# Moving one of two weighted-value sums to an earlier step, splitting a placement, and reordering the sums by bank, in a fused thresholded-attention and squared-ReLU kernel

## The chip, the core and the metric

The kernel runs on one core of one Trainium2 chip. The metric is device time in microseconds (us), the median of repeated runs; lower is better. The core has a matrix engine (PE), a vector engine (DVE), a scalar engine (ACT), a general-purpose engine (POOL), a queue that only issues transfers (SP), and 16 DMA engines. Each engine works through its own instructions in the order of the program, and waits on semaphores for the others.

## What is computed

```python
scores = 0.125 * q @ k^T                       # 8 batches x 8 heads, 576 x 576, head_dim 64
scores = where(scores >= rowmax(scores) - tau, scores, -1e9)
attn   = exp(scores - rowmax) / sum            # softmax over what is kept
x      = (attn @ v), heads side by side        # 4608 x 512
out    = relu(x @ w_in)**2 @ w_out             # 512 -> 2048 -> 512
```

All data are float32.

## The kernel before

**Visits and steps.** The two heads of a pair share one *visit*; there are 32 pairs (8 batches of 4), and so 36 visits, as the first four pairs are visited twice. From visit 12 on, visits go two by two: an even visit n and the odd visit n+1 belong together, and make a *period* of nine *steps*. A step handles 128 query rows of both heads. Step s of a period holds the 64 leftover rows of both visits, steps s+1 to s+4 the blocks 0 to 3 of visit n, and steps s+5 to s+8 the blocks 0 to 3 of visit n+1. There are twelve such periods, run by `late_step`. The score matmuls of two blocks are done at once (L282), at s, s+1, s+3, s+5 and s+7.

**What a step does.** Scores into PSUM banks 0 to 4 (PE, L282); the row maximum (DVE, L303); the exponential (ACT, L318); threshold and sum (DVE, L330); division (POOL, L340). One step later, `turn_blocks` transposes the block in squares of 32 x 32 on DVE into one of two halves of the tile `turned` (L420). Then `place_blocks` has SP issue 16 transfers of 72 KB or 36 KB each that copy these squares to their places in `wT`, the transposed weights (L432 for the block pairs 0 and 1, L437 for the leftover rows). A placement is written (visit, 0), (visit, 1), or (n, 2) for the leftover rows. A period thus has five placements, 80 transfers, all on SP in program order.

**The value sums.** `mix` multiplies `wT` with the values `vs` (PE, L482): 20 matmuls that gather 320 columns in bank 0 (*one*) and 256 columns in bank 4 (*two*). *One* reads the columns ONE of `wT` (block pair 0) and a leftover strip next to them, LEFT for even visits and ODD for odd ones; *two* reads the columns TWO (block pair 1). `put` then copies the sums to `xT` on ACT (L469, L465). `wT` exists once: a placement into ONE has to wait until the last `mix` that reads ONE is done.

**The order around the change.** The step at which a `mix` runs is in `mixes`; the one at which a placement is issued is in `place_at`. In before, `mix` of visit n runs at the beginning of step s+8, and `mix` of n+1 at the beginning of s+11, which is s+2 of the next period. Placements: (n,2) at s+2, (n,0) at s+3, (n,1) at s+5, (n+1,0) at s+8, (n+1,1) at s+9.

**Filling.** All other time of PE goes to *pieces* of the second half of the computation, the two large products with `w_in` and `w_out` (L638, L744), each 1.76 us by the planner's constant `PIECE_US`. `rate` works out how many a step should take, and `fill` issues a quarter of them at a time. A step with a `mix` gets fewer pieces, by `VALUES_US`. An even step puts its scores first, then the turning, the maxima and pieces; an odd step its maxima, then a `mix` if there is one, the turning and pieces. The ring `xT` holds 1280 tokens, and `put` must not overwrite tokens that are still to be read (`read_to`).

Of the kernel before, what the change touches and what calls it, by code (L numbers as in the profile page):

```python
# [19 lines left out]
def kernel(  # L20
# [11 lines left out]
    B, H, S, D = q.shape  # L32
# [3 lines left out]
    HP = H // 2  # L36
    NPAIR = B * HP
    NBLK = S // P
# [51 lines left out]
    RING = 5 * TCH  # L90
# [105 lines left out]
    def some_loads():  # L196
        for _ in range(min(1 + (len(loads) > 8), len(loads))):
            to, src = loads.popleft()
            (nc.gpsimd if state["step"] > first_dma + 2 else nc.sync).dma_start(out=to, in_=src)

    def arrived(t):
        assert all(x[0].tensor.name != t.tensor.name for x in loads)
# [144 lines left out]
    def take(what, among):  # L347
        used[what] += 1
        return bank[among[used[what] % len(among)]]
# [98 lines left out]
    read_to = {"x": 0}  # L448
# [30 lines left out]
    def mix(n, cols):  # L479

        def term(ps, u, c, at, rows=slice(0, P), first=False, last=False):
            nc.tensor.matmul(ps[u * D:(u + 1) * D, :], vs[n % 2][rows, u * (NBLK + 1) + c, :],  # L482
                             wT[rows, NBLK if c == NBLK else u * (NBLK + 1) + c, at:at + ps.shape[1]],
                             start=first, stop=last)

        above, below = slice(0, D), slice(D, P)
        arrived(vs[n % 2])
        if not by_dma(n):
            ps = take("tx", (4, 5))[:, 0:cols.stop - cols.start]
            for c in range(NBLK):  # L490
                for u in range(2):
                    term(ps, u, c, cols.start, first=(c == 0))
            for u, rows in enumerate((above, below)):
                term(ps, u, NBLK, cols.start, rows, last=True)
            put(n, cols.start, ps, False)
            return
        n1, n2 = 2 * P + REST, 2 * P
        at = ODD if paired(n) and n % 2 else ONE
        one, two = bank[0], bank[4]
        groups = (one[:, 0:n1], at, (above, below)), (two[:, 0:n2], TWO, (below, above))  # L500
        for c in range(NBLK):
            for ps, x, _ in groups:
                for u in range(2):
                    term(ps, u, c, x, first=(c == 0))

        for ps, x, places in groups:
            for u, rows in enumerate(places):
                term(ps, u, NBLK, x, rows, last=True)
        put(n, 0, one[:, ONE - at:ONE - at + 2 * P], True)
        left = ODD if at == ODD else LEFT - at  # L510
        put(n, NBLK * P, one[:, left:left + REST], False)
        put(n, 2 * P, two[:, 0:n2], True)
# [85 lines left out]
    def some_later(engine):  # L598
        if later[engine]:
            make(*later[engine].popleft())  # L600
# [191 lines left out]
    visits = [(g_, list(range(FIRST))) for g_ in range(HP)] + [(g_, list(range(FIRST, NBLK + 1))) for g_ in range(HP)]  # L792
    visits += [(g_, list(range(NBLK + 1))) for g_ in range(HP, NPAIR)]

    def paired(n):

        return n >= 3 * HP
# [7 lines left out]
    def by_dma(n):  # L805

        return n >= 3 * HP - 1
# [5 lines left out]
    mixes = {}  # L813
    complete = {}
    for s, (n, i) in enumerate(steps):

        if by_dma(n):
            mixed = {visits[n][1][-1]: (0, 3 if n % 2 else 4)}
        else:
            mixed = {x: (x, 3) for x in range(NBLK + 1)}  # L820
        if i in mixed:
            first, lag = mixed[i]
            cols = slice(first * P, S if by_dma(n) else min((i + 1) * P, S))
            mixes[s + lag] = (n, cols)
            g_ = visits[n][0]
            if g_ % HP == HP - 1:
                complete[s + lag] = g_ // HP * S + cols.stop
    END = max(mixes)

    chunk_at, j = {}, 0  # L830
# [29 lines left out]
    def add_chunk(j):  # L860
        waiting.extend(pieces_of(j))
        whole.add(j)
# [25 lines left out]
    def after():  # L888
        now = state["last"]
        state["last"] = []  # L890
        for fn in state["then"]:
            state["last"] += fn() or []
        state["then"] = []
        for fn in now:
            fn()

    def piece():
        _, fn, *what = waiting.popleft()
        state["left"] -= PIECE_US
        if fn is mlp_out or what[0] <= PLAIN and what[1] == 0:  # L900
            after()
        then = fn(*what)
        after()
        state["then"] = then
        if state["step"] >= NST:
            some_later("vector")
            some_later("gpsimd")

    def fill(us):
        state["left"] += us  # L910
        while waiting and state["left"] >= PIECE_US / 2 and waiting[0][0] <= state["usable"]:
            piece()
        state["left"] = min(state["left"], PIECE_US)

    pieces, left = [], n_pieces
    for s, (n, i) in enumerate(steps):
        if s < HP * FIRST:
            x = int(n > 0 and i == 0)
        else:
            x = 2 if (n, i) in ((2 * HP - 2, FIRST + 1), (2 * HP - 1, FIRST + 1), (2 * HP, FIRST)) else 1  # L920
# [13 lines left out]
    place_at, load_at, prep_at = ({s: [] for s in range(END + 10)} for x in range(3))  # L934
    for s, (n, i) in enumerate(steps):
        if not by_dma(n) or i != visits[n][1][0] or paired(n) and n % 2:
            continue
        nxt = n + (2 if paired(n) else 1)
        more = nxt < len(visits)
        if paired(n):  # L940

            place_at[s + 2].append((n, 2))
            place_at[s + 3].append((n, 0))
            place_at[s + 5].append((n, 1))
            place_at[s + 8].append((n + 1, 0))
            place_at[s + 9].append((n + 1, 1))
            prep_at[s].append(lambda n=n: prep_part(q, n))
            load_at[s].append(lambda n=n: load_part(q, n + 1))
            load_at[s + 2].append(lambda n=n: load_v(n))
            prep_at[s + 4].append(lambda n=n: prep_part(q, n + 1))  # L950
            load_at[s + 4].append(lambda n=n: load_v(n + 1))
        else:
            place_at[s + 3].append((n, 0))
            place_at[s + 4].append((n, 1))
            place_at[s + 5].append((n, 2))
        if more:
            a, b, c, d = (s + 1, s + 5, s + 7, s + 8) if paired(n) else (s + 1, s + 2, s + 4, s + 4)
            load_at[a].append(lambda n=nxt: load_part(k, n))
            if paired(n):
                load_at[a].append(lambda n=nxt: load_left(n))  # L960
            prep_at[b].append(lambda n=nxt: prep_part(k, n))
            load_at[b].append(lambda n=nxt: load_part(k, n + 1))
            if not paired(n):
                load_at[s - 8].append(lambda n=nxt: load_left(n))
            load_at[b].append(lambda n=nxt: load_part(q, n))
            prep_at[c].append(prep_left)
            prep_at[d].append(lambda n=nxt: prep_part(k, n + 1))
# [16 lines left out]
    def turn_last(s):  # L984
        if s <= NST:
            turn_blocks(*steps[s - 1])
        for what in place_at[s]:
            place_blocks(*what)

    def late_step(s):  # L990

        on = s < NST
        odd = on and steps[s][1] % 2 == 1
        if on:
            n, i = steps[s]
            if not odd:
                scores_of_two(s)
                turn_last(s)
            maxima(s, [area(u, odd) for u in range(2)])
            after()  # L1000
            some_later("gpsimd")
            exponents(n, i)
        if s in mixes:
            mix(*mixes[s])
            for j in chunk_at.get(s, ()):
                add_chunk(j)
        if odd or not on:
            turn_last(s)
        quarter = rate(s) / 4 if s < END else 1e9
        fill(quarter)  # L1010
        some_later("vector")
        some_later("gpsimd")
        smooth = s not in mixes
        if smooth:
            after()
        if on:
            threshold(n, i)
            for fn in prep_at[s] + load_at[s]:
                fn()
            divide(n, i)  # L1020
        if smooth:
            fill(quarter)
            after()
            some_later("gpsimd")
        some_loads()
        some_later("vector")
        if not smooth:
            some_later("gpsimd")
            fill(quarter)
        some_loads()  # L1030
        fill(quarter)
        some_loads()
        fill(quarter)
        some_loads()

    for s in range(END + 1):
# [9 lines left out]
        if on:  # L1046
            n, i = steps[s]
# [49 lines left out]
        smooth = s > first_dma + 2 and s not in mixes  # L1097
# [23 lines left out]
        if 0 < s <= NST and by_dma(steps[s - 1][0]):  # L1121
            m, x = steps[s - 1]
# [57 lines left out]
```

## Time and profile before

The time is 1424.66 us, the median of 3 runs (1424.31 to 1427.45). The profiled execution spans 1423.4 us. Its stages on PE:

| stretch | length | PE busy | mean granted clock | what runs |
|---|---|---|---|---|
| 0 to 290 us | 290 us | 257.7 us | mixed | first visits, rounding of weights |
| 290 to 1273 us | 983 us | 920.2 us | 0.98 | the twelve periods, with pieces |
| 1273 to 1423 us | 150 us | 146.8 us | 1.00 | pieces alone |

The other engines in the middle stretch: DVE busy for 703.1 us, POOL for 718.9, ACT for 374.8. PE is the engine with the least idle time, and so the table is read from its side: in the middle stretch it stands for 62.8 us in which it does nothing, and the granted clock, a share of its full speed, shows whether it was slowed besides.

### The profile page before, as it was taken

The page shows a single profiled execution, that of the slowest core. Times are in us where ns is not written, and L with a number is a line of the kernel's source. Part 1 is how long each engine was busy: PE and PEld are TensorE (multiplying, and loading weights), DVE is VectorE, ACT ScalarE, POOL GpSimd, SP SyncE. Part 2 cuts the span into 40 slices and gives each one's busy share as a digit, 9 for nine tenths or more (in the row PEclk, how much of TensorE's full clock was granted, in tenths as well). Part 3 has the DMA queues.
Part 4 walks back from the last instruction along what each step waited for, and adds up shares of the span by engine and source line. Part 5 has one row for each costly group of instructions (what it writes and reads, how often), then busy time and mean ns, then how long its engine had stood idle before and what let it go on. Part 6 is the DMA issues. An engine that isn't in the chain of part 4 may idle for free.

```text
span 1423.4 us, 25861 instructions
## 1 busy us (share of the span) xinstructions
PE 1324.7 (93%) x9112; PEld 1092.6 (77%) x9112; DVE 949.0 (67%) x2026; ACT 582.5 (41%) x1357; POOL 976.4 (69%) x1229
## 2 busy tenths in 40 slices
PE   7899999799898989989998999989989998999998
PEld 5676567577686868778787878877777876889998
DVE  6877776667685877757886777858677767722232
ACT  4777673225252524325342444333425252513322
POOL 3688874696776859595978686868685766652451
PEclk8999999999999999999999999999999999999999
DMA  7754431444646555544646555454645436240000
GB/s 151 162 157 138 118 73 36 80 91 85 108 85 98 115 93 112 87 94 82 115 81 116 99 108 102 87 88 87 107 97 89 91 74 105 59 82 1 16 16 16
DMA packets 406354, 128.15 MB, mean 90 GB/s; under 512 B 390064, under 2 KB 394448, under 8 KB 406224
## 3 DMA queue, kind: packets, MB, share of 16 engines
q1 hardware_dynamic: 385632, 95.10, 37.3%
q0 software_dynamic: 18288, 31.11, 8.3%
q8 instruction: 72, 1.18, 0.4%
q10 hardware_dynamic: 2304, 0.29, 0.2%
q14 instruction: 58, 0.48, 0.1%
HBM read 50.59 MB, written 9.44 MB: 42 GB/s over the span
## 4 chain that ended last, share of the span: by engine, by line
PE 61%; SPq 13%; POOL 10%; DVE 5%; issue 4%; ACT 4%; DMA 3%; ACTq 0%; DVEq 0%; POOLq 0%
PE big L744 18%; PE big L638 18%; SPq L432 11%; PE big L482 10%; PE big L282 5%; PE big L530 3%; PE big L266 3%; DMA wT<-turned 3%; POOL w L340 2%; POOL g L569 2%; PE big L709 2%; PE big L380 2%; DVE w L330 1%; DVE st L303 1%; DVE turned L420 1%
## 5 line engine op out<-in xcount | busy, mean ns | idle before, releaser
L303 DVE TENSOR_REDUCE st<-big 128x1 f32<-128x576 f32 x288 | 203.5, 745 | 92.4 <-PE big L282 58.3
L420 DVE STREAM_TRANSPOSE turned<-w 128x512 f32<-128x512 f32 (+2 forms) x388 | 174.8, 499 | 122.1 <-POOL w L340 64.4
L340 POOL TENSOR_SCALAR w<-w,st 128x576 f32<-128x576 f32 x269 | 233.8, 878 | 24.0 <-DVE st L333 17.3
L330 DVE SCALAR_TENSOR_TENSOR w<-big,st,w 128x576 f32<-128x576 f32 x269 | 208.2, 810 | 56.8 <-ACT w L318 56.5
L744 PE MATMUL big<-wo,gsum 128*128 128x256 f32 x1088 | 244.5, 382 | 0.0
L482 PE MATMUL big<-wT,vs 128*64 128x128 f32 (+7 forms) x1700 | 189.1, 381 | 56.9 <-issue 28.2
L744 PEld LDWEIGHTS big<-wo,gsum 128*128 128x128 f32 x1088 | 204.5, 190 | 36.7 <-issue 9.5
L482 PEld LDWEIGHTS big<-wT,vs 128*64 128x64 f32 (+1 forms) x1700 | 107.6, 145 | 134.2 <-issue 77.6
L638 PE MATMUL big<-xT,w_in_sb 128*128 128x128 f32 x1536 | 187.7, 277 | 8.0 <-DVE g L650 6.4
L338 POOL TENSOR_SCALAR st<-st 128x2 f32<-128x2 f32 (+1 forms) x148 | 33.8, 229 | 234.3 <-DVE w L330 227.3
L638 PEld LDWEIGHTS big<-xT,w_in_sb 128*128 128x128 f32 x1536 | 179.1, 192 | 16.1 <-DVE g L650 7.7
L744 PE MATMUL big<-wo,g 128*128 128x256 f32 x816 | 186.2, 382 | 0.5 <-ACT g L646 0.5
L318 ACT ACTIVATE w<-big,st 128x576 f32<-128x576 f32 x269 | 183.6, 733 | 0.2 <-ACT st L316 0.2
L744 PEld LDWEIGHTS big<-wo,g 128*128 128x128 f32 x816 | 151.4, 190 | 27.3 <-issue 7.9
L315 ACT ACTIVATE st<-st 128x2 f32<-128x2 f32 (+1 forms) x148 | 30.2, 204 | 268.6 <-DVE st L303 267.5
L650 DVE TENSOR_TENSOR g<-big,g 128x512 f32<-128x512 f32 x96 | 64.7, 677 | 76.5 <-PE big L638 71.5
L282 PE MATMUL big<-kT,qT 64*128 64x256 f32 (+3 forms) x768 | 107.5, 416 | 0.7 <-DVE qT L240 0.6
L282 PEld LDWEIGHTS big<-kT,qT 64*128 64x128 f32 x768 | 84.7, 187 | 15.5 <-issue 7.5
L646 ACT ACTIVATE g<-g 128x512 f32<-128x512 f32 x96 | 60.5, 630 | 77.2 <-DVE g L650 77.1
L520 POOL TENSOR_TENSOR gsum<-g 128x512 f32<-128x512 f32 x34 | 44.2, 1301 | 61.0 <-ACT g L647 60.7
L647 ACT ACTIVATE g<-g 128x512 f32<-128x512 f32 x128 | 80.7, 630 | 4.1
L638 PE MATMUL big<-xT,gsum 128*128 128x128 f32 x512 | 65.1, 281 | 4.2 <-POOL gsum L569 3.8
(114 smaller groups left out, 2136.8 us busy)
## 6 DMA issues: line engine op xcount, KB each, us to landing
wT<-turned SPq DMA_DIRECT2D x800, 72.0 KB, 2.2
wo<-in_moe_w_in_dram SPq DMA_DIRECT2D x16, 512.0 KB, 4.5
wo<-in_moe_w_out_dram SPq DMA_DIRECT2D x16, 512.0 KB, 3.6
out_dram<-osb POOLq DMA_DIRECT2D x32, 256.0 KB, 2.5
ql<-in_q_dram POOLq DMA_DIRECT2D x96, 72.0 KB, 2.9
wT<-turned SPq DMA_DIRECT2D x192, 36.0 KB, 2.0
kl<-in_k_dram POOLq DMA_DIRECT2D x88, 72.0 KB, 3.0
vs<-in_v_dram POOLq DMA_DIRECT2D x48, 128.0 KB, 3.2
```

What stands on the lines that cost most here:

```text
L282: nc.tensor.matmul(big[to, at + x0:at + x1], lhsT, keys[u * D:(u + 1) * D, x0:x1], start=True, stop=True)
L303: nc.vector.tensor_reduce(out=mx[:, u:u + 1], in_=sc[u], axis=AX.XY, op=ALU.max)
L318: nc.scalar.activation(out=w[:, u, :].rearrange("p (h k) -> p h k", h=2), in_=sc[u], func=AF.Exp, bias=bias[:, u:u + 1], scale=SCALE)
L330: nc.vector.scalar_tensor_tensor(out=wu, in0=sc[u], scalar=thr[:, u:u + 1], in1=wu, op0=ALU.is_ge, op1=ALU.mult, accum_out=sm[:, u:u + 1])
L340: nc.gpsimd.tensor_scalar(out=w[:, u, :], in0=w[:, u, :], scalar1=z[:, u:u + 1], scalar2=rcp[:, u:u + 1], op0=ALU.add, op1=ALU.mult)
L420: nc.vector.transpose(wb[:, at:at + k1 - k0, i % 2, :], w[:, u, k0 * 32:k1 * 32].rearrange("p (k q) -> p k q", q=32))
L432: nc.sync.dma_start(out=to[:, :, at:at + 64], in_=wb[rows, j::4, :, :].rearrange("p c u q -> p c (u q)"))
L482: nc.tensor.matmul(ps[u * D:(u + 1) * D, :], vs[n % 2][rows, u * (NBLK + 1) + c, :], wT[rows, NBLK if c == NBLK else u * (NBLK + 1) + c, a ...
L638: nc.tensor.matmul(to[:, f, :], factor(j, p, q, c)[:, f * P:(f + 1) * P], part[:, c, :], start=(p in "125" and f == 0 and c == 0), stop=(p ...
L647: nc.scalar.activation(out=to, in_=to, func=AF.Square)
L650: nc.vector.tensor_tensor(out=x, in0=to, in1=x, op=ALU.add)
L744: nc.tensor.matmul(to, left[:, f, :], wo[:, slot, f, :], start=(f == 0), stop=(f == HF - 1))
```

## The change

Four edits. (1) `mix` of an even visit moves from the beginning of step s+8 to the end of step s+6, ahead of the last quarter of the pieces; the same place in its step is taken by `mix` of visit 11, the unpaired visit ahead of the periods. A loop ahead of it runs pieces until the ring `xT` has room. (2) Placement (n+1,0) moves from s+8 to s+7, right after the turning of its second block. (3) Placement (n,2) is split: the half that goes to LEFT is issued at s+1, the half that goes to ODD at s+2 (both at s+3 in the first period). (4) Within `mix`, all of *one*'s matmuls over the four whole key blocks are done ahead of *two*'s, in place of taking turns. The aim is that a transfer is issued as soon as its squares are turned.

```diff
-        for c in range(NBLK):
-            for ps, x, _ in groups:
+        for ps, x, _ in groups:
+            for c in range(NBLK):
                 for u in range(2):
                     term(ps, u, c, x, first=(c == 0))
...
-            mixed = {visits[n][1][-1]: (0, 3 if n % 2 else 4)}
+            mixed = {visits[n][1][-1]: (0, 3 if n % 2 else 2)}
...
-            place_at[s + 2].append((n, 2))
+            a, b = (1, 2) if paired(n - 1) else (3, 3)
+            place_at[s + a].append((n, 2, (0, 1)))
+            place_at[s + b].append((n, 2, (2, 3)))
...
-            place_at[s + 8].append((n + 1, 0))
+            place_at[s + 7].append((n + 1, 0))
...
-        if s in mixes:
-            mix(*mixes[s])
-            for j in chunk_at.get(s, ()):
-                add_chunk(j)
+        def values():
+            if s in mixes:
+                while (visits[mixes[s][0]][0] // HP + 1) * S - RING > read_to["x"]:
+                    piece()
+                mix(*mixes[s])
+                for j in chunk_at.get(s, ()):
+                    add_chunk(j)
+
+        at_end = s in mixes and (mixes[s][0] % 2 == 0 or not paired(mixes[s][0]))
+        if not at_end:
+            values()
...
-        smooth = s not in mixes
+        smooth = at_end or s not in mixes
...
+        if at_end:
+            values()
         fill(quarter)
```

## The prediction

> **What bounds the kernel now.** I start with the page's busy shares, the group of the value sums, and the chain that ended last.
>
> ```profile
> PE 1324.7 (93%) x9112; PEld 1092.6 (77%) x9112; DVE 949.0 (67%) x2026; ACT 582.5 (41%) x1357; POOL 976.4 (69%) x1229
> ...
> PE 61%; SPq 13%; POOL 10%; DVE 5%; issue 4%; ACT 4%; DMA 3%; ACTq 0%; DVEq 0%; POOLq 0%
> ...
> L482 PE MATMUL big<-wT,vs 128*64 128x128 f32 (+7 forms) x1700 | 189.1, 381 | 56.9 <-issue 28.2 <-DMA wT<-turned 12.2 <-DVE w L330 9.1
> ```
>
> PE is busy 93% of the span, so of 98.7 us of idle time 56.9 lie ahead of L482. SP, which computes nothing, holds 13% of the chain: the issuing of transfers is on the path. The waits of PE and of the SP queue say which:
>
> ```profile
> PE big L482 <- issue: 28.2, 8, 5.5
> PE big L482 <- DMA wT<-turned: 9.7, 3, 4.1
> ```
>
> ```profile
> SPq L432 <- DVE turned L420: 149.0, 27, 12.6
> SPq L432 <- PE big L482: 141.4, 12, 15.0
> ```
>
> The first pair is PE's list from 290 to 1273 us; adding 2.9 (DVE L330) and 1.8 (DVE L782), PE waits there 42.6 us for value sums. The second pair shows twelve waits of SP for a value sum, one in each period. The timelines of PE and SP around one period's end join them:
>
> ```profile
> 741.74 4.79 PE L482 MATMUL big<-wT,vs 128*64 128x320 f32 x40
> ```
>
> ```profile
> 746.55 11.22 SPq L432 DMA_DIRECT2D wT<-turned  x16
> ```
>
> ```profile
> 757.88 10.69 SPq L432 DMA_DIRECT2D wT<-turned  x16
> ```
>
> ```profile
> 766.10 0.76 PE L482 MATMUL big<-wT,vs 128*64 128x320 f32 x4
> 770.93 5.94 PE L482 MATMUL big<-wT,vs 128*64 128x256 f32 x36 [4.08 <-DMA wT<-turned]
> ```
>
> The even sum runs freely and ends at 746.5; only then may SP place (n+1,0) over ONE, for 11.2 us, and (n+1,1) behind it, for 10.7 us, to 768.6. The last transfer lands about 2.2 us later, and the odd sum, which reached *two* at 766.9, stands until 770.93. The cycle "even sum, 22 us of issuing, 2.2 us, odd sum" is longer than the work PE has between. The same gap ahead of *two* is in all twelve odd sums: 4.06, 4.67, 4.43, 5.45, 1.81, 4.08, 1.69, 4.07, 1.83, 1.98, 3.79 and 1.85 us, together 39.7. The long ones cost twice, as the clock in windows around this sum shows (length, busy shares, clock, DMA):
>
> ```profile
> 766.10:770.93 4.83, 0.76 (x4) 0.22 (x5) 1.00 0.93 176
> 770.93:774.90 3.97, 3.97 (x20) 2.57 (x22) 0.57 0.61 123
> 774.90:776.90 2.00, 1.97 (x20) 0.80 (x16) 1.00 0.20 30
> ```
>
> For some 3.4 us after the wait PE is granted half its clock. Behind the eight gaps of 3.79 us and more it is 6.8 us four times (the first four) and 3.4 us four times, behind the gaps under 2 us almost never: 40.8 us at half rate, or 20.4 us lost.
>
> **What the Trainium skill says.** "TensorE: Matmul & The Clock Gate", section "HAM oscillation — how this bites in real kernels", warns of idle gaps of PE over about 3.4 us, and counts the loss as half of the throttled time. This trace agrees: gaps under 2 us are free of it, those from 3.79 us are not. "DMA: Bandwidth & Descriptors", section "Anatomy of one DMA — SWDGE (gpsimd) path", says that DMA engines wait for no semaphore: the waiting is done by the issuing sequencer ahead of dispatch. The 12 waits of SP agree: everything behind a blocked placement stands too. It puts a transfer's fixed cost at about 2.0 us; here the page's median to landing is 2.2.
>
> **The change, part by part.**
>
> *Even sum two steps earlier, (n+1,0) at s+7.* In the period above the second block of (n+1,0) is turned by 731.6, yet its placement begins at 746.55. With the even sum done at about s+7 (732.5 here), it runs about 733 to 744, and SP is free before the last turning of n+1 is done, 2 us behind the start of s+9 (median; at 750.1 here). So (n+1,1) is issued from 752 to 763 and landed at 765, where *two* of the odd sum is reached at 766.9. The twelve gaps of 39.7 us close, and their clock loss of 20.4 us with them: **-60.1 us**. The 2.9 us ahead of two odd sums for L330 stay.
>
> *What the even sum now waits for.* It needs (n,1), which is issued behind the turning at s+5. From the timelines, the landing (end of issue plus 2.2 us) comes after the start of the scores of s+5 by, period by period: 19.5, 16.3, 17.1, 16.3, 15.7, 15.1, 13.1, 13.8, 12.9, 14.3, 18.3 and 14.6 us. The built order of the changed kernel puts between those scores and the sum five pieces, four in periods 2 and 3, eight in 5 (room in the ring). With scores of 2.2 us, a piece of 1.78 and 2.1 us for *one*'s eight matmuls (320 columns, 4.79 us over 20 matmuls scaled by width), *two* is reached at 2.2 + 8.9 + 2.1 = 13.2 us; with four pieces at 11.4, with eight at 18.5. The waits are the differences: 6.3, 4.9, 5.7, 3.1, 0, 1.9, 0, 0.6, 0, 1.1, 5.1, 1.4: **+30 us**. Four are over 3.8 us and should bring the half clock, at 3.4 to 6.8 us a time: **+10 us** (7 to 14). Low bound for all: 5 us, if DVE, no longer held by late landings (32.5 us in its waits for `wT<-turned`), turns two microseconds sooner. High bound: 60 us, if PE, running faster, outruns DVE by 2 us more in each period.
>
> *Scores right behind the sum.* In eight periods, and behind visit 11's sum, no piece is left between the even sum and the scores of s+7, which write into banks 0 and 4. ACT's copies to `xT` have to come first: behind the sum that ended at 746.53 they ran
>
> ```profile
> 746.60 0.37 ACT L469 COPY xT<-big 128x256 f32<-128x256 f32 x1 [2.20 <-PE big L482]
> 746.87 0.22 ACT L465 COPY xT<-big 128x64 f32<-128x64 f32 x1
> ```
>
> so bank 0 is free 0.6 us after the sum; with the semaphore about 0.7 us of idle PE, nine times: **+6 us**. On ACT nothing urgent is queued behind the waiting copy: the next exponentials need those very scores. DVE and POOL do not wait for it directly.
>
> *Split of (n,2).* Its LEFT half (8 transfers, 5.5 us) goes out while SP otherwise waits for the odd sum; the ODD half follows that sum as before. SP is not the bound then: nothing, hidden behind pieces until (n,0) is turned.
>
> *One bank, then the other.* Same 20 matmuls; *two* is reached 2.1 us after the beginning in place of 0.8. I have counted it in the slack of both sums. The order of landing asked of *one* changes nothing, as ONE lands first. For visit 11 it costs: LEFT lands last there (284.8 us), and now the whole sum waits, about +3 us, partly at half clock.
>
> Sum: -60 + 30 + 10 + 6 + 3 = -11; I take off some of the +30, since the large waits of periods 1 to 4 and 11 were measured with DVE held up by late landings, and say **-16 us: 1408.5 us**.
>
> **Rivals.** (A) The even sum hardly waits: 5 us in place of 40. For it: in periods 7 to 9 the difference is 0 to 0.6. Against it: period 11 has the same small odd gap as 6, 8 and 10 and a late landing all the same. It gives -60 + 5 + 9 = -46, 1379 us. (B) The wait moves and grows: with PE faster, the chain from scores to turned squares over DVE, ACT and POOL (about 32 us from the scores of s+3 to landing, against 29.7 us of PE work to *two*) becomes the bound in each period. At the high bound of 60 us of waits, 20 of clock and 9 of the rest, it is +29, 1454 us; half way there, 45 + 15 + 9 - 60 = +9, 1434 us, which I take for this case. For it: DVE and POOL are busy 72 and 73% from 290 to 1273, and POOL L340 holds 64.4 us of DVE's turning. Against it: turning at s+5 comes on average 1.8 us after its scores begin, so not much is behind. (C) The two sides cancel: 1424 to 1427.
>
> **How the numbers follow.** My forecast 57% (1393 to 1421), A 20% (1370 to 1392), B 17% (1428 to 1445), C 6%. Faster: 57 + 20 + a little of C, 0.78; within 0.2% 0.06; slower 0.16. The range reaches from 1382, half of A left out, to 1428.
>
> **What would show it.** Right: PE's wait ahead of *two* gone from the odd sums, and SP's wait for L482 cut from 141 us to below 60; new waits of PE ahead of *two* in even sums, of 0 to 6 us; 0.7 us ahead of the scores at s+7. Wrong: odd sums that still wait; even sums that wait everywhere over 4 us, with a clock below 0.97; or idle time of PE at L638 well above its 19 us.

## The result, and the profile after

The changed kernel takes 1414.46 us (median; 1413.01 to 1417.03) beside 1426.06 us for the kernel before in the same runs: a ratio of 0.9918, 95% interval 0.9893 to 0.9943, or 11.6 us less. The prediction was 1408.5 us, 16 us less, in a range of 1382 to 1428.

The page of the changed kernel, the same lines as of before:

```profile
PE 1326.5 (94%) x9112; PEld 1092.8 (77%) x9112; DVE 952.6 (68%) x2026; ACT 581.3 (41%) x1357; POOL 978.5 (69%) x1229
...
PE 62%; POOL 15%; DVE 7%; SPq 6%; issue 4%; ACT 4%; DMA 3%; ACTq 0%; DVEq 0%; POOLq 0%
...
L482 PE MATMUL big<-wT,vs 128*64 128x128 f32 (+7 forms) x1700 | 180.7, 371 | 35.5 <-DMA wT<-turned 13.0
```

The issuing queue fell from 13% to 6% of the chain, and PE's idle time ahead of value sums from 56.9 to 35.5 us. POOL and DVE took SP's place in the chain (10 to 15%, 5 to 7%). The waits of the SP queue (total, times, longest):

```profile
SPq L432 <- DVE turned L420: 240.7, 42, 12.6
...
SPq L437 <- PE big L482: 49.4, 12, 8.9
SPq L432 <- PE big L482: 20.9, 8, 4.9
```

For the block pairs (L432) SP hardly waits for a value sum any more (141.4 us before); for the leftover rows (L437) it waits somewhat longer than before (37.4 us). Mostly it waits for the squares to be turned (149.0 us before). An odd sum, in the timeline of PE, runs through:

```profile
778.34 4.79 PE L482 MATMUL big<-wT,vs 128*64 128x320 f32 x40 
```

All twelve odd sums do. But an even sum, here that of the second period, now stands where *two* begins:

```profile
404.13 2.37 PE L482 MATMUL big<-wT,vs 128*64 128x320 f32 x16 
412.86 4.33 PE L482 MATMUL big<-wT,vs 128*64 128x256 f32 x24 [6.36 <-DMA wT<-turned]
```

The 16 transfers of (n,1) were issued from 398.0 to 409.4 us; PE waited for the last to land. Windows over this stretch give the clock (each row ends with clock, DMA share and GB/s):

```profile
404.20:412.90 8.70, 2.35 (x19) 1.06 (x19) 6.31 (x15) 2.79 (x6) 8.33 (x14) 0.81 0.67 121
412.90:419.70 6.80, 6.80 (x45) 4.48 (x47) 0.09 (x1) 1.98 (x6) 1.86 (x3) 0.75 0.32 65
```

The clock is 0.81 and 0.75 here: about 6.8 us at half rate, as long as behind the longest odd waits of before. About half of it falls into the wait itself, where PE loses nothing by it.

To compare kernels, I add up four things of each profile from 296 us to its end: PE's idle time ahead of value sums, PE's other idle time, the time at half clock (without a stretch that runs on past the last matmul), and the part of that time in which PE was at work. Half of this last part is lost; the rest of the time at half clock is idle time, which stands in the columns before.

| kernel | us, median | ratio to before, 95% interval | idle ahead of sums | other idle | at half clock | PE at work in it |
|---|---|---|---|---|---|---|
| before | 1426 to 1427 | 1 | 42.6 | 20.2 | 44.4 | 33.1 |
| changed | 1414.5 | 0.9918 (0.9893 to 0.9943) | 20.9 | 27.2 | 34.1 | 28.4 |
| changed, order undone (e1) | 1435.3 | 1.0068 (1.0054 to 1.0083) | 38.3 | 24.7 | 51.2 | 41.1 |
| before, order alone (e2) | 1405.4 | 0.9864 (0.9838 to 0.9890) | 23.7 | 23.4 | 17.1 | 17.1 |
| changed, split undone (e3) | 1413.9 | 0.9918 (0.9906 to 0.9931) | 20.2 | 27.1 | 37.5 | 31.5 |
| changed, charged later (e4) | 1417.8 | 0.9935 (0.9915 to 0.9956) | 3.6 | 48.8 | 27.3 | 25.9 |
| before, bank one whole (e5) | 1394.7 | 0.9783 (0.9758 to 0.9807) | 2.7 | 27.5 | 3.4 | 3.4 |
| changed, bank one whole (e6) | 1417.5 | 0.9941 (0.9918 to 0.9965) | 17.0 | 25.1 | 34.1 | 27.5 |
| changed, two queues (e7) | 1447.8 | 1.0145 (1.0119 to 1.0170) | 42.1 | 26.3 | 61.4 | 53.6 |
| before, leftovers mid (e8) | 1391.3 | 0.9757 (0.9737 to 0.9777) | 4.8 | 25.2 | 17.1 | 16.8 |
| changed, leftovers mid (e9) | 1410.5 | 0.9895 (0.9879 to 0.9911) | 13.4 | 25.6 | 34.1 | 32.0 |

For the change as a whole: sums -21.7, other idle +7.0, clock -(33.1 - 28.4)/2 = -2.3, and +5.4 for scores that stall behind an even sum (0.67 us, eight times; below): -11.6 us. The spans of the two profiles differ by 12.2, the medians by 11.6.

### The profile page after: what moved, and what is told of

It reads as the page before. It is cut to its first block, busy times and chain, and to the rows that moved or that the text cites. A ratio compares the mean times of both kernels' runs of the same rounds, so it can differ in the third digit from the quotient of the medians.

```text
span 1411.2 us, 25854 instructions
## 1 busy us (share of the span) xinstructions
PE 1326.5 (94%) x9112; PEld 1092.8 (77%) x9112; DVE 952.6 (68%) x2026; ACT 581.3 (41%) x1357; POOL 978.5 (69%) x1229
## 3 DMA queue, kind: packets, MB, share of 16 engines
q1 hardware_dynamic: 385632, 95.10, 37.4%
## 4 chain that ended last, share of the span: by engine, by line
PE 62%; POOL 15%; DVE 7%; SPq 6%; issue 4%; ACT 4%; DMA 3%; ACTq 0%; DVEq 0%; POOLq 0%
PE big L638 19%; PE big L744 18%; PE big L482 9%; PE big L282 6%; SPq L432 4%; POOL w L340 3%; PE big L530 3%; PE big L266 3%; POOL g L569 3%; DVE w L330 2%; DMA wT<-turned 2%; PE big L709 2%; PE big L380 2%; DVE st L303 2%; DVE turned L420 1%
## 5 line engine op out<-in xcount | busy, mean ns | idle before, releaser
L330 DVE SCALAR_TENSOR_TENSOR w<-big,st,w 128x576 f32<-128x576 f32 x269 | 208.2, 810 | 52.9 <-ACT w L318 52.7
L744 PE MATMUL big<-wo,gsum 128*128 128x256 f32 x1088 | 243.5, 381 | 0.0
L744 PEld LDWEIGHTS big<-wo,gsum 128*128 128x128 f32 x1088 | 204.7, 190 | 35.7 <-issue 8.0
L482 PE MATMUL big<-wT,vs 128*64 128x128 f32 (+7 forms) x1700 | 180.7, 371 | 35.5 <-DMA wT<-turned 13.0
L638 PE MATMUL big<-xT,w_in_sb 128*128 128x128 f32 x1536 | 191.3, 280 | 8.2 <-ACT g L663 5.1
L638 PEld LDWEIGHTS big<-xT,w_in_sb 128*128 128x128 f32 x1536 | 182.3, 195 | 18.3 <-issue 8.1
L482 PEld LDWEIGHTS big<-wT,vs 128*64 128x64 f32 (+1 forms) x1700 | 101.2, 141 | 109.2 <-issue 47.1
L744 PE MATMUL big<-wo,g 128*128 128x256 f32 x816 | 184.3, 381 | 0.0
L744 PEld LDWEIGHTS big<-wo,g 128*128 128x128 f32 x816 | 151.8, 190 | 22.7 <-issue 3.6
L282 PE MATMUL big<-kT,qT 64*128 64x256 f32 (+3 forms) x768 | 114.1, 422 | 5.6 <-DVE qT L240 4.4
L282 PEld LDWEIGHTS big<-kT,qT 64*128 64x128 f32 x768 | 87.4, 189 | 27.1 <-issue 8.5
L638 PE MATMUL big<-t,g 128*128 128x128 f32 x512 | 64.7, 283 | 7.2 <-POOL g L569 6.3
```

The source lines that it names most:

```text
L282: nc.tensor.matmul(big[to, at + x0:at + x1], lhsT, keys[u * D:(u + 1) * D, x0:x1], start=True, stop=True)
L330: nc.vector.scalar_tensor_tensor(out=wu, in0=sc[u], scalar=thr[:, u:u + 1], in1=wu, op0=ALU.is_ge, op1=ALU.mult, accum_out=sm[:, u:u + 1])
L638: nc.tensor.matmul(to[:, f, :], factor(j, p, q, c)[:, f * P:(f + 1) * P], part[:, c, :], start=(p in "125" and f == 0 and c == 0), stop=(p ...
L744: nc.tensor.matmul(to, left[:, f, :], wo[:, slot, f, :], start=(f == 0), stop=(f == HF - 1))
```

## The experiments

### Which edit brings the gain (e1, e2, e3)

e1 takes the order by bank out of the changed kernel:

```diff
-        for ps, x, _ in groups:
-            for c in range(NBLK):
+        for c in range(NBLK):
+            for ps, x, _ in groups:
                 for u in range(2):
                     term(ps, u, c, x, first=(c == 0))
```

> The changed kernel, with the matmuls of one and two taking turns again in every value sum (edit 4 undone); the rest stays. Theory M (the move of the even sum and of placement (n+1,0) closed the odd gaps; what is left is the even sums' wait for the landing of (n,1)): two is reached 0.8 us after a sum's start in place of 2.1, so each even sum that waits now waits 1.3 us longer. Nine of twelve waits in the changed kernel are over zero, so +10 to +12 us of waits and 3 to 7 us of clock: about 1428 us, level with the kernel before; the odd sums still do not wait. Theory O (the gain is mostly the order by bank, the move is a wash): much worse, 1435 to 1445 us, with odd sums that wait again. Theory P (the pace is set by DVE and POOL now, waits at the sums only take up slack): no change, 1414 us.

Measured: 1435.3 us, slower than before by 0.68%. PE's waits in the middle stretch of e1:

```profile
PE big L482 <- DMA wT<-turned: 22.7, 7, 6.4
PE big L482 <- DVE turned L420: 10.9, 2, 7.4
```

The even sums stand 4.76, 6.41, 7.35, 4.10, 0, 3.58, 1.63, 3.17, 0.87, 2.21, 1.56 and 2.25 us, together 37.9, beside 20.9 in the changed kernel. That is 1.4 us more for each on average, near theory M's 1.3, and of the odd sums one waits, 0.42 us, against theory O, which had odd sums wait again. The time, though, lies above M's 1428 and just inside O's 1435 to 1445: the waits grew by 17 us where M expected 10 to 12, and 6.3 us more were lost to the clock, near the upper end of its 3 to 7. So the move with the split, *without* the order by bank, does not gain but lose. It turned 42.6 us of waits at sums, nearly all odd ones, into 38.3 at even ones; other idle time grew by 4.5, the clock loss by 4.0, and the scores behind even sums stall as in the changed kernel, some 6 us.

e2 puts the same edit alone into the kernel before.

```diff
-        for c in range(NBLK):
-            for ps, x, _ in groups:
+        for ps, x, _ in groups:
+            for c in range(NBLK):
```

> The kernel before, with edit 4 alone: one's matmuls ahead of two's. The twelve odd sums reach two 1.3 us later, so their gaps of 1.69 to 5.45 us should shrink by 1.3 us each: 39.7 - 15.6 = 24 us. Only one or two gaps stay above 3.8 us, so most of the 20.4 us lost to the half clock goes too. Theory M: the order alone is worth the 15.6 us of gaps and 10 to 17 us of clock, so 1394 to 1401 us, faster than the changed kernel; the move then costs something on top. Theory O says the same and puts all of the gain there. Theory P: the gaps close at two and open at another place; 1420 us or above.

Measured: 1405.4 us, 1.36% less than before and some 9 us less than the whole change, though 4 us above the 1401 that M allowed. The waits of PE for its sums in the middle stretch:

```profile
PE big L482 <- issue: 19.1, 11, 3.1
...
PE big L482 <- DMA wT<-turned: 2.5, 1, 2.5
```

The gaps ahead of *two* of the twelve odd sums that had 39.7 us are 3.08, 1.95, 2.85, 2.96, 0.71, 2.51, 0.33, 2.89, 1.50, 0.20, 2.26 and 0.37: together 21.6, at most 3.08 (24 were expected), and the time at half clock fell from 44.4 to 17.1 us. By the columns that is -18.9 + 3.2 - 8.0 = -23.7 us; the spans of the profiles differ by 23.3 and the medians by 20.9. The six runs of e2 lie between 1399.5 and 1410.7 us, the three quickest with a mean clock of 0.985, the slowest with 0.979, and the profile is of a quick one. Pieces take 3.8 us longer in sum, but only because 10.5 us of them fell into stretches at half clock, beside 3.1 before: at full clock they come to 819.8 and 819.7 us.

e3 makes the placement of the leftover rows whole again, at s+2 (s+3 in the first period).

```diff
-            a, b = (1, 2) if paired(n - 1) else (3, 3)
-            place_at[s + a].append((n, 2, (0, 1)))
-            place_at[s + b].append((n, 2, (2, 3)))
+            place_at[s + (2 if paired(n - 1) else 3)].append((n, 2))
```

> The changed kernel, with placement (n,2) whole again at s+2 (s+3 in the first period); the rest stays. Theory M, as in the prediction: the split is worth nothing, as SP is not the bound there; 1413 to 1416 us, with the same waits at the sums. Rival: the early half keeps (n,0) and through it the later turnings on time; without it SP ends (n,2) 5 us later, (n,0) and the turning of (n,1) come later by up to 5 us, and the even waits grow by 1 to 3 us each: 1420 to 1440 us.

Measured: 1413.9 us, the same ratio to before as the whole change, with idle times within 1 us. In the changed kernel the split is worth nothing, as expected by M.

Together: order alone -1.4%, move with split alone +0.7%, both -0.8%. The whole gain is the order's, and the move gives some of it back. Edits 1 and 2, the moves of the even sum and of (n+1,0), were not taken apart.

### Where the even wait goes if it is filled (e4)

e4 has the planner charge the time of an even sum to the step after it, so that more pieces come ahead of the sum.

```diff
-        us = VALUES_US if s in mixes and by_dma(mixes[s][0]) else 0.0
+        us = 0.0
+        for x, even in ((s, 0), (s - 1, 1)):
+            if x in mixes and by_dma(mixes[x][0]) and (paired(mixes[x][0]) and mixes[x][0] % 2 == 0) == even:
+                us += VALUES_US
```

> The changed kernel, with the time of an even sum charged by the planner to the step after it. By the built order the even sum is then preceded by two more pieces (3.6 us) in its step and followed by one or two ahead of the scores of s+7, with as many fewer in step s+7; total work is the same. Theory M: two is reached 3.6 us later, so of the even waits of 3.1, 6.4, 5.7, 2.4 and 1.6 us some 14 us go, with their half clock of about 10 us, and the 0.7 us stalls of the scores behind the sum (8 times) go too: 14 + 8 + 5 = 27 us less, 1388 us. The scores of s+7 and the turning of s+9 come nearer to each other, which may bring waits of 0 to 2 us at odd sums: 1388 to 1400 us. Theory P: 1410 to 1416 us, as DVE and POOL set the pace.

Measured: 1417.8 us, no gain, though the waits did as M said: 0.68, 1.89 and 1.02 us are left at even sums, none elsewhere, and in the periods no scores stand directly behind an even sum. But PE's other idle time grew from 27.2 to 48.8 us. Its waits in the middle stretch of e4:

```profile
PE big L638 <- DVE g L650: 9.9, 6, 3.1
...
PE big L744 <- ACT g L646: 3.7, 1, 3.7
PE big L638 <- DVE osb L782: 3.4, 1, 3.4
PE big L744 <- ACT held L757: 3.2, 2, 2.4
PE big L744 <- DVE gsum L764: 3.0, 1, 3.0
```

L744 did not wait in the changed kernel. The new gaps (3.70, 2.41, 3.02, 3.01, 3.41, 2.50 and 3.12 us) stand in seven of the periods within 8 us ahead of the scores of s+9. Here a piece waits for its operands from DVE and ACT. The likely reason is that the pieces taken from step s+7 had given these engines the time to work off the scores of s+7; this was not tested apart. So M was right on the wait and wrong on the time. The time lies just above the 1410 to 1416 us of theory P, and the new waits are of its kind, though for DVE and ACT in place of DVE and POOL: a us taken from the even sum's wait is not a us of time.

### Does the issuing of (n,1) set the wait (e7)

e7 gives the last 4 of the 16 transfers of each (n,1) to the ACT queue.

```diff
-                    nc.sync.dma_start(out=to[:, :, at:at + 64], in_=wb[rows, j::4, :, :].rearrange("p c u q -> p c (u q)"))
+                    queue = nc.scalar if qb == 3 and pair == 1 and paired(vis) and vis % 2 == 0 else nc.sync
+                    queue.dma_start(out=to[:, :, at:at + 64], in_=wb[rows, j::4, :, :].rearrange("p c u q -> p c (u q)"))
```

> The changed kernel, with the last 4 of the 16 transfers of each placement (n,1) issued by ACT in place of SP. Theory M (an even sum waits for the issuing of (n,1)): SP ends 2.7 us sooner, so of the even waits of 3.08, 6.36, 5.67, 2.42 and 1.63 us and the small ones about 14 us go and about half of the clock lost there (7 us). Against it ACT gives 4 issues to a period, at most 2.5 us ahead of the exponentials of s+5. 1394 to 1402 us. Rival (the wait is for the turning on DVE, or for the copies to xT, not for the issuing): waits as they are, 1414 us or more.

Measured: 1447.8 us, a miss of both theories: the even waits doubled. The waits of the SP queue show a new entry near the top, and ACT's timeline in one period shows its four issues:

```profile
SPq L433 <- DMA wT<-turned: 136.8, 15, 16.8
```

```profile
823.01 2.63 ACTq L433 DMA_DIRECT2D wT<-turned  x4
```

In this period SP issues the last but two of (n,0) at 816.4 us and then stands until 825.8, 2.8 us behind the issue of ACT's first transfer. Its wait is for a transfer's landing: the transfer it issues at 825.82 counts on the same semaphore as ACT's first, which landed at 825.80. The transfers of both queues share eight semaphores in turn. SP ended (n,1) at 835.6, the last landing is at 838.11, and *two* began at 838.52. So the test did not shorten the issuing; it delayed it, and the sum followed the landing within half a us. That fits M, but the direct test of a quicker issuing was not had.

### Freeing ONE earlier (e5, e6, e8, e9)

e2 had left 21.6 us of odd gaps. If they are the fixed chain of the prediction (last read of ONE, issuing, landing), an earlier last read shortens them. e5 finishes bank one, leftover keys included, ahead of bank two, in the kernel before:

```diff
-        for c in range(NBLK):
-            for ps, x, _ in groups:
-                for u in range(2):
-                    term(ps, u, c, x, first=(c == 0))
-
         for ps, x, places in groups:
+            for c in range(NBLK):
+                for u in range(2):
+                    term(ps, u, c, x, first=(c == 0))
             for u, rows in enumerate(places):
                 term(ps, u, NBLK, x, rows, last=True)
```

> The kernel before, with bank one finished whole (the four key blocks and the leftover keys) ahead of all of bank two's matmuls, in both sums; no move, no split. Theory W (the odd gap is a fixed chain: last read of ONE by the even sum, 22 us of issuing, 2.2 us, two of the odd sum; each us cut from it is a us of gap): ONE is free after 10 matmuls (2.7 us) in place of 20 (4.8), and two of the odd sum is reached 0.5 us later than with the order by bank alone, so 2.6 us of each of its gaps go: of the 21.6 us measured there (3.08 at most, eleven below 3) about 20, and the 8 us of clock. 1405 - 20 - 4 to 8 = 1377 to 1381 us. Rival (DVE and POOL set the pace below some 1400 us): the gaps at two close, others at L638 and L744 open by as much; 1400 to 1406 us.

e6 is the same edit in the changed kernel.

> The changed kernel, with bank one finished whole ahead of bank two. Theory W: its odd sums do not wait, so the earlier free ONE is worth nothing to them; its even sums wait for (n,1), and two is reached 0.5 us later: eight waiting sums, 4 us, with some clock: 1408 to 1411 us, so 25 to 30 us slower than the same order in the kernel before. Rival (the earlier placement of (n+1,0) and its early turning help the later steps): below 1400 us.

Measured: e5 1394.7 us, e6 1417.5. In e5 the odd gaps are gone but for 0.67, 0.61 and 1.45 us, and the half clock with them (3.4 us). The time lies between the 1377 to 1381 us of theory W, and the 1400 to 1406 of its rival. One cause of what W missed is seen in the timeline of PE, a sum without a wait in e5:

```profile
835.10 5.52 PE L482 MATMUL big<-wT,vs 128*64 128x320 f32 x40 
```

5.5 us in place of 4.8. The starts of its matmuls tell why. With the four leftover matmuls (64 rows each) next to each other, all four start within 0.02 us, at different corners of the array, and the next pass of all four 0.3 us on; with bank one finished whole they run two and two. Over 25 sums that is some 18 us. e8 keeps the early end of *one* and brings the four together: one's four key blocks, one's leftovers, two's leftovers, two's key blocks.

```diff
+        for part, (ps, x, places) in enumerate(groups):
+            for c in list(range(NBLK)) + [NBLK] if part == 0 else [NBLK] + list(range(NBLK)):
+                for u, rows in enumerate(places):
+                    ends = c == (0, NBLK)[part], c == (NBLK, NBLK - 1)[part]
+                    term(ps, u, c, x, rows if c == NBLK else slice(0, P), *ends)
```

> The kernel before, with each sum in the order: one's four key blocks, one's leftover keys, two's leftover keys, two's four key blocks; no move, no split. ONE is free after 10 matmuls as with bank one finished whole, but the four leftover matmuls (64 rows each) stand together again, where the trace shows them starting within 0.02 us of each other; with the bank finished whole they ran two and two, and a sum took 5.5 us in place of 4.8. Theory Q (that 0.7 us in 25 sums, 17 us, is what that version lost): sums of 4.8 us, the gaps at two as small as there (under 5 us together), 1376 to 1381 us. Rival (DVE and POOL set the pace near 1395): 1392 to 1398 us, with the 17 us turned into waits at L638 and L744.

e9 is the same order in the changed kernel.

> The changed kernel with the same order inside each sum. Theory M: its sums are 4.8 us long, its even sums reach two as late as in the changed kernel, and an earlier free ONE is worth nothing to odd sums that do not wait: 1411 to 1417 us, 30 us or more behind the same order without the move. Rival (the moved even sum is no worse once SP is quick enough): within 10 us of the version without the move.

Measured: e8 1391.3 us, e9 1410.5. A sum of e8:

```profile
832.93 4.94 PE L482 MATMUL big<-wT,vs 128*64 128x320 f32 x40 
```

4.9 us again, 14 us less than e5 over 25 sums, but only 6 us of them reach the spans of the profiles and 3 the medians, which puts e8 just under the 1392 to 1398 us of theory Q's rival and well above Q's 1376 to 1381. Waits at sums are up by 2.1 us, as with quicker sums PE is sooner at *two*, and the loss to the clock by 6.7. This second part does not arise at the sums: none of e8's five stretches at half clock stands at one or right behind it. Four of them stand behind waits of pieces (L635) of 1.88 to 2.86 us. e5 has seven waits of pieces of 1.86 to 2.30 us, only one of which was followed by half clock (the last section tells what decides). e8 has the lowest median of all versions, 2.4% under before and 1.6% under the changed kernel; the interval of its ratio overlaps that of e5.

With the move, e6 was expected at 1408 to 1411 us and took 1417.5; e9 was expected at 1411 to 1417 and took 1410.5. Both lie less far behind the same order without the move than was foreseen (25 to 30 us, and over 30), and both are outside what the rivals had (below 1400, and within 10 us). And in each of four orders inside the sum, the move (with its split) is slower than no move: by 9 us (1435.3 against 1426.3), 9 (1414.5 against 1405.4), 23 (e6 against e5) and 19 (e9 against e8).

## Why the prediction was right, and where it was not

*The odd gaps close: right.* All twelve are gone, with the 2.9 us for L330 that were to stay. SP's wait for L482 at L432 fell to 20.9 us, under the 60 foreseen.

*The even sums wait for (n,1): right in kind, the size somewhat high.* Expected 6.3, 4.9, 5.7, 3.1, 0, 1.9, 0, 0.6, 0, 1.1, 5.1, 1.4; measured 3.08, 6.36, 5.67, 2.42, 0, 0.23, 0.27, 1.63, 0, 0.57, 0, 0.66. The sum is 20.9 in place of 30, or of the 25 to which the total of -16 comes down. The eleventh period was the largest miss; its long way from scores to landing in the kernel before did not come again.

*Clock: the term that was too good.* The prediction took off 20.4 us and put back 10. It counted half of the whole time at half clock as lost, but PE had been idle in part of it, and that part is in the gaps already: of the 40.8 us behind odd sums PE worked in 29.7, so 14.8 us were lost. The measured loss from 296 us on went from 16.5 to 14.2 us, 2.3 less instead of 10.4. Two readings of the gaps were wrong besides: there are seven of 3.79 us and more, not eight, and the gap of 1.98 us was followed by 3.4 us at half clock, so gaps under 2 us are not always free of it. Nor does the line of about 3.4 us that the prediction names hold here: in the changed kernel a single wait of 2.42 us (up to 575.8 us) was followed by half clock. Of the 34.1 us at half clock after, 6.8 each are behind the two longest even waits; but some stand behind gaps of 2.0 to 2.9 us or behind several shorter ones, and one (310.5 us) behind a wait of 4.44 us of the scores L282 for DVE, which no step of the prediction had.

*Scores behind a sum: right.* In the timeline of PE of the changed kernel:

```profile
741.24 2.63 PE L482 MATMUL big<-wT,vs 128*64 128x256 f32 x24 [0.23 <-issue]
743.80 2.89 PE L282 MATMUL big<-kT,qT 64*128 64x256 f32 x16 
```

These scores last 2.89 us in place of 2.21, seven times in the periods (once 2.95), and once behind visit 11's sum, 0.67 us of stall each; an eighth period waits otherwise. It shows as busy time, not as idle time. Expected was 0.7, nine times. e6 and e9 bear out the cause: there bank one is done before the sum's end and its copies can run early (at 743.56 us beside a sum that ends at 745.94 in e6), and scores behind an even sum mostly take 2.31 us.

*Split and visit 11.* The split is worth nothing (e3), as said. Visit 11's sum ended at 292.2 us, as before; the +3 us did not come.

*Other idle time: the term that was missing.* It grew by 7.0 us, 4.4 of them the wait of L282 above, whose cause stays open; at L638 it went only from 19.0 to 21.3 us. Of the rivals, (B) was wrong for the whole change; e4, where shorter even waits came with new waits for DVE and ACT, is the one run that fits its mechanism.

*The step that failed: "One bank, then the other".* The prediction put this edit at nothing of its own, inside the slack of both sums, and gave the whole -16 us to the move. The runs give the order -20 us alone and the move with its split about +9. The numbers for it were in the prediction: 1.3 us more to *two* against twelve gaps of 1.69 to 5.45 us, the long ones with a clock loss. Worked out alone it would have given -15.6 us for the gaps and a part of the clock loss; measured were -18.1 and -8.0. The waits of the even sums did use the order (*two* at 2.1 us and not at 0.8), so the total was made for both edits at once; the story of which edit earned it was wrong. That the total came so near is luck besides: waits that came out smaller than forecast made up for a clock gain that was too large and for idle time that had no term.

What stays open: whether a quicker issuing of (n,1) would remove the even wait, as the test of it delayed the issuing.

## What to carry to other kernels

Where a consumer reads several transfers that land one after the other, order its reads by landing: 1.3 us more of work ahead of the last operand, in each of twelve sums, took 18 us off the waits and 8 off the clock loss, and the time fell by 21. Moving a consumer earlier to break one wait pays only if its own operand lands early enough: here the even sum came ahead of the landing of (n,1), whose turning and 11 us of issuing had not moved, and the wait went from the odd to the even sum. When idle time and a slower clock are added up, count the slower clock only where the engine is at work. Cost edits one by one even when they come together, since two of opposite sign can add up to the right total.

## What the hardware showed besides

- What brings the half clock is not the length of a gap alone. In all eleven profiles the stretches at half clock begin and end on a grid of 3.41 us, which lies differently in each profile. Between 300 and 1260 us, 62 of the grid's stretches at full clock had PE idle for 2.0 us or more, and each of them was followed by one at half clock; of 45 with 1.6 to 2.0 us of idle time 21 were; of 2863 with less, none. So a gap counts by how much of it falls into one stretch. In e2 the gap of 3.08 us was cut in two by the grid and cost nothing, while that of 2.51 us lay in one stretch and was followed by half clock (length, PE busy, clock, DMA):

```profile
364.15:367.57 3.42, 1.68 (x14) 1.00 0.67 109
367.57:370.98 3.41, 2.07 (x20) 1.00 0.80 149
370.98:374.39 3.41, 3.41 (x22) 1.00 0.41 60
760.10:763.51 3.41, 0.90 (x8) 1.00 0.69 122
763.51:766.92 3.41, 3.41 (x20) 0.50 0.65 125
```

- A part of the clock loss is thus likely to be chance, as the grid lies differently each time: the six runs of e2, one kernel, had mean clocks of 0.979 to 0.985. A few us of this loss, from one profile, say little about an edit.
- Four matmuls of 64 rows and 64 columns at different corners of the array start within 0.02 us of each other when they are neighbours in the program. Set two and two, the 20 matmuls of a sum took 5.5 us in place of 4.8.
- In e7 a transfer on ACT's queue held up SP's queue for 9 us in the period shown, as both count on semaphores used in turn.
